# Sparse attention and routed experts on one Trainium2 core: more transposes by DMA, some near rows issued by GpSimd, expert 1's loads released

## The chip, the cores and the metric

The kernel runs on one core of a Trainium2 chip. The core has five engines that run side by side and are tied together by semaphores: TensorE (matmuls and transposes, PE in the profile), VectorE (DVE), ScalarE (ACT), GpSimd (POOL) and SyncE (SP, which here only issues DMAs). Each takes its own instructions in program order. DMAs are issued by an engine and carried out by 16 DMA engines that all queues share. The metric is the device time of one execution in microseconds (us).

## The reference

Two stages. Attention over 4 batches, 8 heads, 768 positions, head dimension 64: every query sees the keys less than 16 positions away, and beside them 24 block summaries (the maximum of the keys and the mean of the values over blocks of 32):

```python
k_sum = k.reshape(B, H, nb, block, D).max(axis=3)
v_sum = v.reshape(B, H, nb, block, D).mean(axis=3)
scores_l = scale * np.matmul(q, k.transpose(0, 1, 3, 2))
mask_l = np.abs(pos[:, None] - pos[None, :]) < window
scores_s = scale * np.einsum('bhsd,bhnd->bhsn', q, k_sum) + np.log(block)
scores_all = np.concatenate([np.where(mask_l, scores_l, -1e9), scores_s], axis=-1)
a = np.exp(scores_all - max); a = a / (sum + 1e-09)
out = np.matmul(a, np.concatenate([v, v_sum], axis=2))
```

Its output is reshaped to x of 3072 tokens by 512. Then eight experts on all tokens, weighted by a table P that is normalised over rows and columns eight times:

```python
P = np.exp(logits - logits.max())            # logits = x @ w_gate
for _ in range(8):
    P /= P.sum(1, keepdims=True) + 1e-09; P /= P.sum(0, keepdims=True) + 1e-09; P *= N / E
for e in range(E):
    out += P[:, e:e + 1] * (np.maximum(x @ w1[e], 0.0) @ w2[e])
```

## The kernel before

*Pairs.* Attention is done for 16 pairs of heads, i = 0 to 15, four to a batch. Pairs 0 to 3 are taken in halves. From pair 4 on, a pair is one unit of work (`pair_start` and `pair_whole`), and these pairs are what the change touches. A pair goes through these steps:

- GpSimd issues the loads of its keys and queries (`load_qk`, tiles kst and qst, two DMAs each) and of its values (`load_v`, tile vx). They cast from float32 to bfloat16.
- Keys and queries are transposed into kT and qT. Up to pair 11 TensorE does it (`tr`, L305, six 128x128 transposes each) and ScalarE or VectorE copies the result out of PSUM. From pair 12 on SyncE issues a DMA transpose from SBUF to SBUF (`tr_dma`, L310).
- `key_max` and `block_sums` make the block summaries; `block_out` writes the summary values into rows 0 to 63 of the tile Ve.
- `near_values` copies, with four small DMAs (L362, L364), the 16 first and last rows of each block of 128 values into rows 64 to 127 of Ve, where they serve as the neighbours across the block's edge. SyncE issues them.
- `scores` (L334, two halves), `score_exp`, `masks`, `edges` and `summary_exp` make the weights; `values` (two halves) makes the weighted sums: six matmuls of a block with its own values (L406, tile vx), then three that add summaries and near rows (L412, tile Ve). `normalize` divides.
- The outputs go into xT, the transposed input of the experts: by TensorE and a copy (`to_xT`, L517, and `x_out`), for pairs 10 to 14 by a DMA transpose of SyncE (`x_dma`, L314).

*Expert 0* starts while attention still runs: `expert0` works on 384 tokens at a time, in eight hidden tiles of four matmuls each (`hidden_mm`, L200) and three projections of eight matmuls (`project_mm`, L210, each issued as two halves). They fill TensorE between the steps of attention.

*The order.* The kernel is scheduled by its own planner, class `Plan`, when the program is built. Every step is a unit with an engine, a cost, what it depends on, a priority and a lag: the time after its end until its result is taken to be there. The planner gives each engine a fixed order of instructions from these numbers; the hardware then runs each engine's order as it stands, and a unit that is early or late in reality doesn't change it. In this order expert 0's tiles stand between units of attention on TensorE.

*GpSimd's loads* form a chain of their own (`load`, with `last[0]`): pair after pair, then expert 1's weights, four pieces of w1 (`load_w1`, L176, two DMAs of 128 KB each) and w2 (`load_w2`, L187, 1 MB). In front of expert 1's stands a hold (L818 to L822): four one-element copies of GpSimd that read qT of pairs 12 to 15, and so wait until the DMA transposes of these pairs have landed. Tile pools set other waits: V_e has two buffers, so near rows of pair i wait for the weighted sums of pair i-2; vx has six, so the values of pair 15 wait for the sums of pair 9.

*After attention* the routing table is normalised beside the rest of expert 0 and the first group of expert 1; then experts 1 to 7 run through a fixed loop up to the end of the kernel. The planner's part ends at about 170 us.

The units that the change re-plans, in the version before:

```python
if i >= 12:
    U["tr", i, z] = U["kT", i, z] = add("SP", 1.25, lambda z=z: tr_dma(i, z), ...)
...
if 10 <= i < 15:
    U["xt", i] = U["x", i] = add("SP", 1.25, lambda: x_dma(i), ...)
```

Of the kernel before, what the change touches and what calls it, by code (L numbers as in the profile page):

```python
# [10 lines left out]
BF16 = mybir.dt.bfloat16  # L11
# [22 lines left out]
class Plan:  # L34
# [12 lines left out]
    def add(self, eng, cost, fn, deps=(), prio=0.0, opens=(), uses=(), lag=0.0):  # L47
        u = Unit(eng, cost, fn, [d for d in deps if d is not None], prio, list(opens), lag)
        for b in list(opens) + list(uses):
            b.users.append(u)  # L50
        if uses and eng != "PE":
            u.prio -= 100.0
        self.waiting.append(u)
        return u
# [62 lines left out]
def kernel(  # L117
# [10 lines left out]
    nc = tc.nc  # L128

    B, H, S, D = q.shape  # L130
    G = S // 128
# [6 lines left out]
    NP = (B * H) // 2  # L138
    PB = H // 2
    SCALE = 1.0 / float(D) ** 0.5  # L140
    W = 16
# [4 lines left out]
    VD = D + 1  # L146
# [68 lines left out]
    NB = PB  # L215
    NE = 2
# [7 lines left out]
    attn = early.enter_context(tc.tile_pool(name="attn", bufs=1))  # L224
    aps = early.enter_context(tc.tile_pool(name="aps", bufs=1, space=PSUM))
    if True:

        ident = attn.tile([128, 128], BF16, name="ident")
        held = attn.tile([1, 1], BF16, name="held")
        band = attn.tile([128, LIVE], BF16, name="band")  # L230
        m_blk = attn.tile([128, G, 64], BF16, name="m_blk")
        qT = [attn.tile([128, W + S + W], BF16, name=f"qT{i}") for i in range(NB)]
        kT = [attn.tile([128, S], BF16, name=f"kT{i}") for i in range(NB)]
# [10 lines left out]
        add = plan.add  # L244
# [51 lines left out]
        def tr(i, z, tag):  # L296
            st = at.pop(("st", i, z))
            t = at["t", i, z] = bank(tag, "tkq", BF16)
            for g in range(G):
                if i < PB:  # L300
                    for j in range(2):
                        nc.tensor.transpose(t[64 * j:64 * j + 64, g * 128:(g + 1) * 128],
                                            st[:, j, g, :], ident)
                else:
                    nc.tensor.transpose(t[:, g * 128:(g + 1) * 128],  # L305
                                        st[:, g, :, :].rearrange("p j d -> p (j d)"), ident)

        def tr_dma(i, z):
            r, st = i % NB, at.pop(("st", i, z))
            nc.sync.dma_start_transpose(out=(kT[r][:], qT[r][:, W:W + S])[z].rearrange("c (g t) -> c g t", g=G),  # L310
                                        in_=st[:].rearrange("p g j d -> p (g j d)"))
# [45 lines left out]
        def near_values(i):  # L357

            sv, ve = v_x[i % NQ], V_e[i % NE]
            for j in range(2):  # L360
                c0, q0 = VD * j, 64 + 32 * j
                nc.sync.dma_start(out=ve[q0 + W:q0 + 2 * W, 1:G, c0:c0 + VD],  # L362
                                  in_=sv[128 - W:128, j, 0:G - 1, :])
                nc.sync.dma_start(out=ve[q0:q0 + W, 0:G - 1, c0:c0 + VD],  # L364
                                  in_=sv[0:W, j, 1:G, :])

        def scores(i, h):
            sg = at["sg", i, h] = banks2("sg")
            for s in range(HG):
                for j in range(2):  # L370
                    score_mm(i, sg[:, j, s * LIVE:(s + 1) * LIVE], j, HG * h + s, 0, LIVE)
# [244 lines left out]
        U = {}  # L616
        last = [None, None]
# [19 lines left out]
        def pair_start(i, prio):  # L637
            o = i - NB
            war_k = [U.get(("S", o, 0)), U.get(("S", o, 1)), U.get(("km", o))]
            war_q = war_k[:2] + [U.get(("ss", o, 0)), U.get(("ss", o, 1))]  # L640
            tag = "m" if i < PB else "a"
            for z in range(2 if i >= PB else 1):
                if i >= 12:
                    U["tr", i, z] = U["kT", i, z] = add("SP", 1.25, lambda z=z: tr_dma(i, z),
                                                        [U["kq"[z], i]] + (war_k, war_q)[z], prio, lag=5.0)
                    continue
                buf = Buffer(tag)
                U["tr", i, z] = add("PE", 0.4, lambda z=z: tr(i, z, tag),
                                    [U["kq"[z], i], U["ident"]] + (war_k, war_q)[z]
                                    + [U["tr", i, 0] if z else U.get(("S", i - 1, 1 if i > PB else 0))],  # L650
                                    prio, opens=[buf])
                U["kT", i, z] = add({"ACT": 0.8} if z == 0 else {"ACT": 0.8, "DVE": 0.95},
                                    0, lambda z=z: tr_out(U["kT", i, z].on, i, z), [U["tr", i, z]], prio,
                                    uses=[buf])
            if i < PB:
                query_half(i, 0, prio)
            U["km", i] = add("DVE", 0.95, lambda: key_max(i), [U["kT", i, 0]] + war_q[2:], prio)
            buf = Buffer("a")
            U["vs", i] = add("PE", 0.4, lambda: block_sums(i),
                             [U["v", i]] + ([U.get(("A", i - NE, 1))] if i >= PB else []), prio + 0.01, opens=[buf])  # L660
            U["Vs", i] = add("DVE", 0.36 if i < PB else 0.84, lambda: block_out(i), [U["vs", i]],
                             prio + 0.01, uses=[buf])
# [37 lines left out]
            return U.get((what, n % PB, n // PB)) if n >= 0 else None  # L700

        def pair_whole(i, prio):
            U["near", i] = add("SP", 2.5, lambda: near_values(i), [U["v", i], U.get(("A", i - NE, 1))], prio,
                               lag=1.9)
            for h in range(2):
                buf = Buffer("s")
                U["S", i, h] = add("PE", 0.28, lambda h=h: scores(i, h),
                                   [U["kT", i, 0], U["kT", i, 1], U.get(("ed", i - 2))], prio, opens=[buf])
                U["X", i, h] = add("ACT", 0.97, lambda h=h: score_exp(i, h), [U["S", i, h]], prio, uses=[buf])
                U["mk", i, h] = add("DVE", 0.56, lambda h=h: masks(i, h),  # L710
                                    [U["X", i, h], U.get(("A", i - 2, 1))], prio)
            U["ed", i] = add("DVE", 0.78, lambda: edges(i),
                             [U["X", i, 0], U["X", i, 1], U["mk", i, 1], U.get(("A", i - NE, 1))], prio)
            bufs = [Buffer("a"), Buffer("a")]
            U["ss", i, 0] = U["ss", i, 1] = add("PE", 0.22, lambda: summaries2(i),
                                                [U["km", i], U["kT", i, 1], U.get(("A", i - NE, 1))], prio,
                                                opens=bufs)
            for h in range(2):
                U["sx", i, h] = add("ACT", 0.46, lambda h=h: summary_exp(i, h), [U["ss", i, h]], prio,
                                    uses=[bufs[h]])  # L720
            for h in range(2):
                buf = Buffer("a")
                U["A", i, h] = add("PE", 0.4, lambda h=h: values(i, h),
                                   [U["mk", i, h], U["ed", i], U["sx", i, h], U["Vs", i], U["near", i]],
                                   prio, opens=[buf])
                U["no", i, h] = add("DVE", 0.68, lambda h=h: normalize(i, h),
                                    [U["A", i, h], U.get(("xt", i - 2))], prio, uses=[buf])
            if 10 <= i < 15:
                U["xt", i] = U["x", i] = add("SP", 1.25, lambda: x_dma(i), [U["no", i, 0], U["no", i, 1]], prio,
                                             lag=4.5)  # L730
            else:
                buf = Buffer("a")
                U["xt", i] = add("PE", 0.35, lambda: to_xT(i), [U["no", i, 0], U["no", i, 1]], prio, opens=[buf])
                U["x", i] = add({"ACT": 0.8, "DVE": 0.9}, 0, lambda: x_out(U["x", i].on, i), [U["xt", i]], prio,
                                uses=[buf])
# [55 lines left out]
        c0 = add("DVE", 3.8, constants, [], -5.0)  # L791
# [11 lines left out]
        for i in range(PB, NP):  # L803
# [3 lines left out]
            if i % PB == PB - 1:  # L807
# [7 lines left out]
                    zero.extend(U["w2d"])  # L815
                expert0(b * S, xs)
                expert0(b * S + HS, xs)
        def hold():  # L818
            for r in range(12 % NB, NB):
                nc.gpsimd.tensor_copy(out=held[0:1, 0:1], in_=qT[r][0:1, W:W + 1])  # L820

        last[0] = add("POOL", 0.3, hold, [last[0]] + [U["kT", i, 1] for i in range(12, NP)])  # L822
        for i in range(4):
            load(("w1n", i), lambda i=i: load_w1(1, i), 0.85, 1.3)
        load("w2n", lambda: load_w2(1), 0.85, 5.0)
# [13 lines left out]
    if True:  # L839
# [351 lines left out]
        for n in range(LAG, len(groups)):  # L1191
            g0, q0 = g, q
            g = group(*groups[n])
            q = pair(*groups[n - LAG])
            e, j, i = groups[n]
# [48 lines left out]
        last = [pair(*groups[len(groups) - LAG + n], spare=bool(n % 2), c1_at=c1s[n], tail=True) for n in range(LAG)]  # L1244
# [6 lines left out]
        A, B, C, D = last  # L1251
# [42 lines left out]
```

## Time and profile before

| | |
|---|---|
| median of 3 runs | 676.4 us (675.85 to 677.23) |
| the profiled execution | 675.13 us, its span 673.4 us |
| granted TensorE clock over the span | 0.999 |
| TensorE busy, 26.5 to 116 us | 89.00 of 89.50 us |
| VectorE / ScalarE busy there | 76.33 / 66.43 us |
| GpSimd DMA issues in attention | 0.75 to 1.05 us each |
| SyncE issue of a near row / of a DMA transpose | 0.59 / 1.21 to 1.95 us |
| landing of kT's, qT's, xT's DMA transposes after issue (median, range) | 5.2 (2.7 to 6.0), 3.6 (2.8 to 4.5), 4.9 (2.8 to 8.4) us |
| landing of Ve's near rows after issue | 5.0 (1.9 to 6.7) us |

How to read the lines in what follows. A group or timeline line starts with its time: in a timeline, the start in us from the span's start, then the length, the engine, the source line, the operation, the tile written <- the tiles read, the number of instructions, and in brackets how long the engine had been idle before it and what ended the wait. A q after an engine's name is its sequencer: an SPq or POOL DMA line is the issue of a DMA, not its transfer. The view of stretches gives for each stretch its length and then busy time and number of instructions of PE, of PE's weight loads, of DVE, ACT and POOL, the granted clock, the DMA engines' share and GB/s. The view of waits gives engine, line, what it waited for, us in total, times, and the longest.

### The profile page before, as it was taken

The page shows a single profiled execution, that of the slowest core. Times are in us where ns is not written, and L with a number is a line of the kernel's source. Part 1 is how long each engine was busy: PE and PEld are TensorE (multiplying, and loading weights), DVE is VectorE, ACT ScalarE, POOL GpSimd, SP SyncE. Part 2 cuts the span into 40 slices and gives each one's busy share as a digit, 9 for nine tenths or more (in the row PEclk, how much of TensorE's full clock was granted, in tenths as well). Part 3 has the DMA queues.
Part 4 walks back from the last instruction along what each step waited for, and adds up shares of the span by engine and source line. Part 5 has one row for each costly group of instructions (what it writes and reads, how often), then busy time and mean ns, then how long its engine had stood idle before and what let it go on. Part 6 is the DMA issues. An engine that isn't in the chain of part 4 may idle for free.

```text
span 673.4 us, 13531 instructions
## 1 busy us (share of the span) xinstructions
PE 663.9 (99%) x5111; PEld 434.8 (65%) x5111; DVE 580.2 (86%) x1433; ACT 402.5 (60%) x783; POOL 131.5 (20%) x177
## 2 busy tenths in 40 slices
PE   8999999999999999999999999999999999999996
PEld 4666655555666666666666666666666666666665
DVE  6878889777799988998899988998899889998885
ACT  4777776565777765555655565555555555556552
POOL 8599622122101010201010010101020101100001
PEclk9999999999999999999999999999999999999999
DMA  9999959000513060311422050405031141201224
GB/s 115 190 147 145 151 85 172 2 1 1 79 11 37 1 79 1 36 14 21 59 22 28 1 78 9 40 1 79 1 33 17 20 60 20 30 0 48 82 91 158
DMA packets 124018, 36.46 MB, mean 54 GB/s; under 512 B 110384, under 2 KB 121136, under 8 KB 123952
## 3 DMA queue, kind: packets, MB, share of 16 engines
q0 software_dynamic: 104672, 26.22, 41.8%
q1 hardware_dynamic: 18464, 8.83, 5.6%
q8 instruction: 40, 0.66, 0.4%
q10 hardware_dynamic: 816, 0.54, 0.2%
q14 instruction: 26, 0.21, 0.1%
HBM read 52.45 MB, written 6.29 MB: 87 GB/s over the span
## 4 chain that ended last, share of the span: by engine, by line
PE 93%; DVE 4%; DMA 1%; POOL 1%; issue 1%; ACT 0%; DVEq 0%; ACTq 0%
PE xy L913 36%; PE pg L907 16%; PE pa L907 11%; PE pb L907 11%; PE hps L200 6%; PE yps L210 6%; PE sg L334 1%; DMA kst<-in_k_dram 1%; DVE hf L857 1%; PE tkq L305 1%; PE vs L342 1%; PE av L406 1%; PE av L412 1%; PE ss L430 1%; PE tx L517 0%
## 5 line engine op out<-in xcount | busy, mean ns | idle before, releaser
L913 PEld LDWEIGHTS <-hf 128*128 128x128 f16 x2352 | 230.1, 98 | 95.6 <-issue 0.5
L913 PE MATMUL xy<-w,hf 128*128 128x256 f16 x1312 | 183.4, 273 | 0.0
L913 PE MATMUL xy<-ws,hf 128*128 128x256 f16 x984 | 147.6, 273 | 0.1
L191 ACT ACTIVATE hf<-pg 128x512 f16<-128x512 f32 x84 | 50.2, 597 | 150.8 <-PE pg L907 150.8
L1049 DVE SCALAR_TENSOR_TENSOR out_acc<-xy,P_sb,out_acc 128x512 f32<-128x512 f32 x164 | 115.1, 744 | 2.1 <-PE xy L913 2.1
L854 DVE TENSOR_TENSOR hf<-hf 128x512 f16<-128x512 f16 x252 | 100.3, 424 | 8.8
L907 PE MATMUL pa<-xT,w 128*128 128x512 f16 x336 | 99.9, 379 | 0.0
L907 PEld LDWEIGHTS <-w 128*128 128x128 f16 x672 | 65.8, 98 | 44.4 <-issue 1.1
L857 DVE TENSOR_TENSOR hf<-pb,c 128x512 f16<-128x512 f32 x84 | 58.1, 692 | 38.5 <-PE pb L907 32.4
L176 POOL DMA_DIRECT2D w<-in_moe_w_dram x56 | 41.7, 754 | 220.6 <-PE pg L907 192.0
L907 PEld LDWEIGHTS <-ws 128*128 128x128 f16 x504 | 49.3, 98 | 25.3
L941 ACT COPY c<-pg 128x512 f32<-128x512 f32 x84 | 49.2, 586 | 22.4 <-PE pg L907 22.4
L857 DVE TENSOR_TENSOR hf<-pg,c 128x512 f16<-128x512 f32 x84 | 57.2, 681 | 0.8 <-PE pg L907 0.8
L926 ACT COPY pg<-pa 128x512 f32<-128x512 f32 x84 | 47.9, 570 | 4.8
L191 ACT ACTIVATE hf<-pa 128x512 f16<-128x512 f32 x84 | 50.6, 602 | 0.0
L907 PE MATMUL pg<-xTs,w 128*128 128x512 f16 x168 | 50.0, 379 | 0.2
L907 PE MATMUL pg<-xT,w 128*128 128x512 f16 x168 | 50.0, 379 | 0.1
L907 PE MATMUL pb<-xT,ws 128*128 128x512 f16 x168 | 50.0, 379 | 0.0
L907 PE MATMUL pb<-xTs,ws 128*128 128x512 f16 x168 | 50.0, 379 | 0.0
L907 PE MATMUL pg<-xTs,ws 128*128 128x512 f16 x168 | 50.0, 379 | 0.0
L934 ACT COPY c<-pb 128x512 f32<-128x512 f32 x84 | 49.8, 592 | 0.0
L200 PE MATMUL hps<-xT,w 128*128 128x384 f16 x256 | 48.6, 326 | 0.0
(141 smaller groups left out, 820.1 us busy)
## 6 DMA issues: line engine op xcount, KB each, us to landing
w<-in_moe_w_dram POOLq DMA_DIRECT2D x8, 1024.0 KB, 8.9
w<-in_moe_w_dram POOLq DMA_DIRECT2D x56, 128.0 KB, 3.5
out_dram<-out_acc SPq DMA_DIRECT2D x20, 256.0 KB, 2.0
qst<-in_q_dram POOLq DMA_DIRECT2D x32, 96.0 KB, 5.7
vx<-in_v_dram POOLq DMA_DIRECT2D x16, 192.0 KB, 6.5
kst<-in_k_dram POOLq DMA_DIRECT2D x24, 96.0 KB, 5.9
w<-in_moe_w_dram POOLq DMA_DIRECT2D x2, 512.0 KB, 8.6
kst<-in_k_dram POOLq DMA_DIRECT2D x4, 192.0 KB, 5.1
```

Source lines behind the costliest of these rows:

```text
L176: nc.gpsimd.dma_start(out=t[:, :, h, :], in_=moe_w1[e].rearrange("(dk p) f -> p dk f", p=128)[:, :, f:f + 128])
L191: nc.scalar.activation(out=out, in_=in_, func=AF.Relu, bias=0.0, scale=1.0)
L200: nc.tensor.matmul(hp[:, 0:n], lhsT=w1s[e][:, dk, 128 * f:128 * (f + 1)], rhs=xT[:, dk, t0:t0 + n], start=(dk == 0), stop=(dk == KD - 1))
L210: nc.tensor.matmul(yp[:], lhsT=h[:, f, c * 128:(c + 1) * 128], rhs=w2s[e][:, f, :], start=(f == 0), stop=(f == KF - 1))
L854: nc.vector.tensor_tensor(out=out, in0=in0, in1=in1, op=ALU.subtract)
L857: nc.vector.tensor_tensor(out=out, in0=in0, in1=in1, op=ALU.add)
L907: nc.tensor.matmul(bank[:], lhsT=w[:, dk, :], rhs=x[:, dk, :], start=start and dk == 0, stop=dk == KH - 1, skip_group_check=True)
L913: nc.tensor.matmul(bank, lhsT=a(f)[:, 128 * c:128 * (c + 1)], rhs=w[:, f, :], start=start and f == 0, stop=f == FH - 1, skip_group_check=True)
L926: nc.scalar.copy(out=B["g"][:], in_=B["a"][:])
L934: nc.scalar.copy(out=B["c5"][:], in_=B["b"][:])
L941: nc.scalar.copy(out=B["c2"][:], in_=B["g"][:])
L1049: nc.vector.scalar_tensor_tensor(out=acc, in0=src, scalar=P_sb[:, t, e:e + 1], in1=acc, op0=ALU.mult, op1=ALU.add)
```

## The change

Five edits, all in what the planner is given, and one removed step:

- Keys and queries of pairs 10 and 11 are transposed by DMA as well (before: from pair 12 on); the lag in the plan is 6 (5.0).
- Outputs of pairs 8 and 9 go by DMA transpose as well (before: 10 to 14); lag 5 (4.5).
- Near rows of pairs 12 to 15 are issued by GpSimd instead of SyncE, with a plan cost of 3.6 for the four; the lag of all near rows is 2.2 (1.9).
- The hold in front of expert 1's loads is gone, with its tile.

```diff
-                nc.sync.dma_start(out=ve[q0 + W:q0 + 2 * W, 1:G, c0:c0 + VD],
+                eng = nc.gpsimd if i >= 12 else nc.sync
+                eng.dma_start(out=ve[q0 + W:q0 + 2 * W, 1:G, c0:c0 + VD],
                                   in_=sv[128 - W:128, j, 0:G - 1, :])
-                nc.sync.dma_start(out=ve[q0:q0 + W, 0:G - 1, c0:c0 + VD],
+                eng.dma_start(out=ve[q0:q0 + W, 0:G - 1, c0:c0 + VD],
                                   in_=sv[0:W, j, 1:G, :])
...
-                if i >= 12:
+                if i >= 10:
                     U["tr", i, z] = U["kT", i, z] = add("SP", 1.25, lambda z=z: tr_dma(i, z),
-                                                        [U["kq"[z], i]] + (war_k, war_q)[z], prio, lag=5.0)
+                                                        [U["kq"[z], i]] + (war_k, war_q)[z], prio, lag=6)
...
-            U["near", i] = add("SP", 2.5, lambda: near_values(i), [U["v", i], U.get(("A", i - NE, 1))], prio,
-                               lag=1.9)
+            U["near", i] = add(*(("POOL", 3.6) if i >= 12 else ("SP", 2.5)), lambda: near_values(i),
+                               [U["v", i], U.get(("A", i - NE, 1))], prio, lag=2.2)
...
-            if 10 <= i < 15:
+            if 8 <= i < 15:
                 U["xt", i] = U["x", i] = add("SP", 1.25, lambda: x_dma(i), [U["no", i, 0], U["no", i, 1]], prio,
-                                             lag=4.5)
+                                             lag=5)
...
-        def hold():
-            for r in range(12 % NB, NB):
-                nc.gpsimd.tensor_copy(out=held[0:1, 0:1], in_=qT[r][0:1, W:W + 1])
-
-        last[0] = add("POOL", 0.3, hold, [last[0]] + [U["kT", i, 1] for i in range(12, NP)])
         for i in range(4):
             load(("w1n", i), lambda i=i: load_w1(1, i), 0.85, 1.3)
         load("w2n", lambda: load_w2(1), 0.85, 5.0)
```

With the new numbers the planner also orders the engines anew. On SyncE, from the near rows of pair 8 on, the changed program has: transposes of pair 10, near rows of 9, transposes of 11, near rows of 10, output of 8, transposes of 12 and 13, near rows of 11, output of 9, transposes of 14, output of 10, transposes of 15, outputs of 11 to 14. On GpSimd, after the values of pair 15: the eight w1 loads and the w2 load of expert 1, then the near rows of pairs 12, 13, 14 and 15, then the routing table's steps. On TensorE 36 transposes are gone, and the tiles of expert 0 stand at other places between the units of attention.

More of the change, by code (lines that the diff above doesn't have):

```diff
@@ L228 @@
         ident = attn.tile([128, 128], BF16, name="ident")
-        held = attn.tile([1, 1], BF16, name="held")
         band = attn.tile([128, LIVE], BF16, name="band")
```

## The prediction, made before the changed kernel was run

> **What bounds the kernel now.** I read the busy table first, then the stretch the change touches cut out of the trace, then the waits of TensorE and of GpSimd, then the order of time on the three queues concerned. In the page and in the cut:
>
> ```profile
> PE 663.9 (99%) x5111; PEld 434.8 (65%) x5111; DVE 580.2 (86%) x1433; ACT 402.5 (60%) x783; POOL 131.5 (20%) x177
> ...
> 74.00:116.00 42.00, 42.00 (x443) 24.65 (x440) 37.41 (x102) 30.20 (x51) 12.70 (x19) 1.00 1.19 136
> ```
>
> TensorE is busy in all 42.00 us from 74 to 116 us, where everything that the change touches happens, and at full clock (1.00). It takes its instructions in order and has no gap to give. So work taken from TensorE there shortens the kernel by its own length, and a wait put in front of one of its instructions lengthens it by the whole wait. In the view of who waited for whom, no line of TensorE in this stretch waits for a DMA. GpSimd does:
>
> ```profile
> POOL held L820 <- DMA qT<-qst: 16.1, 4, 7.2
> ```
>
> These 16.1 us are the hold that is taken out. In order of time GpSimd shows its last load of attention, the four copies that hold, and expert 1's loads:
>
> ```profile
> 79.98 1.02 POOL L274 DMA_DIRECT2D vx<-in_v_dram  x1 [2.23 <-PE av L412]
> ...
> 98.00 0.18 POOL L820 COPY held<-qT 1x1 bf16<-1x1 bf16 x1 [7.21 <-DMA qT<-qst]
> 98.46 5.95 POOL L176 DMA_DIRECT2D w<-in_moe_w_dram  x8 [0.28 <-issue]
> 104.34 0.95 POOL L187 DMA_DIRECT2D w<-in_moe_w_dram  x1
> ```
>
> The view of the tile w, cut to these loads, has their way from issue to landing. The longest belongs to the load of w2 (cut to 104.0 to 105.5 us, the last small load shows 5.3 and w2 12.3), so w2 landed at 104.3 + 12.3 = 116.6 us; cut to its own issue, the first one landed in 3.7 us, at 102.1 us:
>
> ```profile
> DMA to landing us min/median/max: 3.7/5.0/12.3
> ```
>
> And TensorE, at the place that matters below, pair 12's weighted sums (the L412 matmuls read Ve, which the near rows fill):
>
> ```profile
> 100.54 0.35 PE L406 MATMUL av<-vx,em 128*128 128x65 bf16 x6
> 100.73 0.34 PE L412 MATMUL av<-Ve,Ee 128*128 128x130 bf16 x3
> ```
>
> There they followed the tile before without a wait: pair 12's near rows were issued by SyncE from 88.64 to 91.15 us, and the tile view of Ve for that window gives 1.9 us to landing.
>
> **What the Trainium skill says.** (1) "DMA: Bandwidth & Descriptors", section on SWDGE, HWDGE and iDMA: GpSimd's descriptors go to a ring of which one context is allocated, while SyncE's go to another queue of the same 16 engines, served in turn. The trace agrees: all GpSimd DMAs stand under one queue, q0, SyncE's under q1. (2) Same page, section "Two DMAs through the same engine are not ordered": within one queue of an engine descriptors start in order. The trace fits: w2, last of nine, took 12.3 us where the first took 3.7. (3) Same page, "Queues, rings and completion order": a completion write lands after every earlier write of its engine, across queues. The trace fits: near rows of SyncE landed in 1.9 us when GpSimd loaded nothing (88 to 92 us) and in 4.4 to 6.1 us beside expert 1's loads (101 to 110 us). (4) "TensorE: Matmul & The Clock Gate", Part 1: after an idle window of about 3.4 us the clock is halved until a busy one has passed. Here TensorE's last matmul starts at 667.91 and ends by 668.5 us; the clock record falls to 0.50 at 672.6 us, 4.1 us later.
>
> **What is taken from TensorE.** By the order of time, from the start of one unit to the next: queries' and keys' transposes of pair 10 took 76.44 to 77.20, 0.76 us; pair 11's 81.97 to 82.65, 0.68 us; the output transposes of pair 8 took 74.81 to 75.14, 0.33 us; pair 9's 81.22 to 81.65, 0.43 us. Sum 2.20 us. The evacuations that go with them (six 128x768 copies on ScalarE and VectorE, 0.56 to 0.80 us each) stood beside a full TensorE, as did the hold's copies, and are worth nothing. If nothing else were late, the gain would be 2.2 us.
>
> **What is put on SyncE.** Six DMA transposes of 1.2 to 1.5 us of issue each, minus the near rows of four pairs (16 issues of 0.6 us). Pair 10's transposes can go at 61.7 us, when near rows of pair 8 are out (61.02 + 0.62) and the loads have landed; with the 4.5 to 5.7 us that pair 12's took, they are there by 70 us and the scores of pair 10 start at about 75.9. Pair 11's go behind near rows of pair 9 (66.2 to 68.7), are there by 77, and are read at about 81. Both hidden. Then near rows of pair 10 (to 76.5), the output of pair 8 (1.3), four transposes of pairs 12 and 13, to about 83.9, and only then near rows of pair 11, against 81.16 in the profile: the last is issued at about 85.8 and, with 4.4 to 6.1 us, lands between 90.2 and 91.9. The sums of pair 11 come, without a wait, at 93.28 - 2.20 - 0.65 (one hidden tile now placed after them) = 90.4. So 0 to 1.5 us may be lost there; I take 0.5.
>
> **What moves on GpSimd.** In the changed program the nine loads of expert 1 stand directly behind the values of pair 15, and the near rows of pairs 12 to 15 stand behind the loads, also on GpSimd. The values of pair 15 wait for the sums of pair 9. On TensorE these now have before them 2.42 us more (a hidden tile 0.65, half a projection 0.86, two score units 0.63, the summaries 0.28) and 1.09 less (transposes of pair 10, outputs of pair 8), so the load goes at 79.98 + 1.33 = 81.3 instead of 79.98; it took 6.5 us to land, so 87.8. The loads are issued from 82.3, their data is queued behind it. In the profile the nine landings ran from 102.1 to 116.6, 14.5 us; with the first one 1 us after the values (the eight small loads landed 1 us apart: 98.46 + 3.7 to 103.6 + 5.3), w2 lands at 88.8 + 14.5 = 103.3. Two bounds: if the values don't hold them up, 18.1 us after the first issue as in the profile (116.6 - 98.46), 100.4; if the seven transposes that SyncE now sends in this time (pair 9's output to pair 11's) rather than three cost their whole size, 4 x 0.197 MB at the 174 GB/s that the cut from 108 to 117 us shows, 4.5 us, 107.8. In the profile both kinds of traffic together moved more than loads alone (211 GB/s from 82 to 84 us against 144 from 58 to 82), so a part of this; I take 105.
>
> Near rows of pair 12 are issued once GpSimd is past the loads, and in the program every GpSimd DMA also waits for the landing of the eighth before it: about 89.5 to 93. Their descriptors then stand in q0 behind w2's, on the same engines. They land with w2, at 105.
>
> Sums of pair 12: in the changed order TensorE has before them 2.20 less and also lacks the last hidden tile (98.17 to 98.82, 0.65 us) and a projection (98.82 to 100.54, 1.72), which come after: it is there at 100.54 - 2.20 - 2.37 = 96.0, or 96.5 with pair 11's half microsecond, and passes L406 at once. L412 waits from 96.2 to 105.1, 8.9 us. Behind it in TensorE's queue stands everything else: scores of pair 14, hidden tiles and projections of expert 0; none can pass, so all 8.9 us are lost. (The 0.5 of pair 11 falls into this wait: the landing does not move with it.) Against the profile: 105.1 - 100.73 = 4.4 late, plus the 2.37 that are still owed, **6.7 us late**. Nothing further adds: the last near row of pair 13 may be issued only when w2 has landed, 105.7, landing at 108, but its sums come 6 us after those of pair 12, at 111; pairs 14 and 15 are issued after the sums of 12 and 13 into an empty ring. Earlier landing of expert 1's weights buys nothing: in the profile no TensorE or VectorE wait names their DMA.
>
> **The clock.** 8.9 us of idle are more than the 4.1 after which the record falls. At the start of the profile the clock was half until 7.03 us, TensorE having begun at 1.05. Half speed for 3.4 (the skill's window) to 6 us after the wait costs half of that, 1.7 to 3.0 us; bound below 0 if the record should not fall. I take 2.0. Sum: 8.7 us. The profiled execution took 675.1 us (span 673.4 and 1.7 around it), so 683.8; the median of the runs is 1.3 higher, 676.4, so **685.1**, and I say 685.
>
> **Rivals.**
> - *Near rows pass the weights* (another ring, or small DMAs interleaved): issued by 93.3, landing in 1.9 to 6.1 us, 95.2 to 99.4, against 96.2. TensorE waits 0 to 3.2 us: -2.2 to +1.0, 674.2 to 677.4, most likely 674.5. This is the faster side; it decides if near rows land by about 98.4. For it: only 10 KB each, and the change's own due time for them is 2.2 us. Against: nine loads in the profile landed strictly one behind the other.
> - *A short wait*: the weights land at the lower bound, 100.4, and the clock falls late or not at all: 100.5 - 100.73 + 2.37 = +2.1, and up to 2 of clock: 678.5 to 680.5. For it: the profile's own 18.1 us. Against: the values of pair 15 ahead, and more transposes beside.
> - *SyncE is what is late*: near rows of pair 12 arrive in time, but those of pair 11, behind four transposes, hold its sums by 1.5: -2.2 + 1.5 = -0.7, 675.7. For it: 4.4 to 6.1 us to landing under load. Against: only true if the first rival is.
>
> **How the numbers follow.** Near rows behind the weights, long wait: 0.75, 680.5 to 690 (680.5 without any clock cost and w2 at 102.8; 107.8 with 3.0 of clock gives +12.5, 688.9). Short wait: 0.08. Near rows pass: 0.12 (0.09 faster, 0.01 the same, 0.02 slower). SyncE late: 0.05 (0.03 faster, 0.02 the same). A measurement of this kernel tells about 0.2%, 1.4 us, from no change. Faster 0.12, same 0.03, slower 0.85. The range 677.5 to 690 leaves out the faster cases (0.17 at most) and the upper tail.
>
> **What would show it.** In the profile of the changed kernel: the near rows of pair 12 issued by GpSimd at 89 to 93 us with 10 us or more to landing; a wait of TensorE at L412 for the DMA Ve<-vx of 5 to 10 us around 96 us; a clock record of 0.50 within it or behind it; SyncE's transposes of pairs 10 and 11 with no TensorE wait behind them; 36 fewer transposes on TensorE. It is wrong if the near rows land within 6 us, or if TensorE has no wait above 2 us between 85 and 110 us.

## The result and the profile after

| | before | after |
|---|---|---|
| median | 676.82 us (675.85 to 679.24, 4 runs) | 696.73 us (696.42 to 698.21, 4 runs) |
| ratio | | 1.0293, 95% interval 1.0262 to 1.0324 |
| the profiled execution: span | 673.4 us | 694.6 us |
| granted TensorE clock over the span | 0.999 | 0.982 |

The changed kernel is slower by 19.9 us. The prediction said slower, at the right place, but by 8.7 us, less than half of it. The busy times of the page and the cut of the stretch from 74 to 116 us, the two views that the prediction began with, now of the changed kernel:

```profile
PE 666.7 (96%) x5075; PEld 434.4 (63%) x5075; DVE 581.1 (84%) x1434; ACT 398.8 (57%) x776; POOL 138.5 (20%) x189
```

```profile
74.00:116.00 42.00, 24.90 (x218) 12.62 (x217) 20.58 (x57) 16.76 (x27) 16.04 (x23) 0.80 1.63 153
```

36 transposes are gone from TensorE (5111 instructions before, 5075 now). But where it was busy in all 42.00 us it now works 24.90, at a mean clock of 0.80, and the DMA engines carry 153 GB/s instead of 136. The view of who waited for whom, TensorE alone, 60 to 140 us:

```profile
PE av L412 <- DMA Ve<-vx: 15.3, 1, 15.3
PE sg L333 <- DMA qT<-qst: 3.6, 1, 3.6
```

And the order of time at those places:

```profile
89.82 0.58 PE L333 MATMUL sg<-qT,kT 64*128 64x160 bf16 x6 [3.60 <-DMA qT<-qst]
...
98.44 0.88 POOL L187 DMA_DIRECT2D w<-in_moe_w_dram  x1 [0.59 <-DMA w<-in_moe_w_dram]
100.11 0.56 POOL L362 DMA_DIRECT2D Ve<-vx  x1 [0.79 <-PE ss L430]
...
102.15 0.35 PE L406 MATMUL av<-vx,em 128*128 128x65 bf16 x6
...
117.83 0.50 PE L412 MATMUL av<-Ve,Ee 128*128 128x130 bf16 x3 [15.33 <-DMA Ve<-vx]
```

The long wait is the one that the prediction described: pair 12's sums, L412, for near rows that GpSimd issued behind expert 1's weights. It lasts 15.3 us instead of 8.9, and it ends at 117.83 us, not at 105.1. The second wait, 3.6 us for the queries of pair 12, was not foreseen at all. The tile views give the ways to landing. First w2 alone, second the four near rows of pair 12, third the values of pair 15 (6.5 us before):

```profile
L187 POOL DMA_DIRECT2D w<-in_moe_w_dram x1: 883/883/883, 98.4 to 98.4; - x1
...
DMA to landing us min/median/max: 18.5/18.5/18.5
```

```profile
DMA to landing us min/median/max: 13.5/15.4/17.0
```

```profile
DMA to landing us min/median/max: 14.3/14.3/14.3
```

So w2, issued at 98.44, landed at 116.9, and the near rows between 117.2 (100.11 + 17.0) and 117.7 (104.18 + 13.5), directly behind it. What made all of it late stands in the chain of work that ended last, cut to this stretch (start, length, what):

```profile
78.30 13.51 DMA kst<-in_k_dram
...
92.10 11.80 DMA w<-in_moe_w_dram
...
104.18 13.51 DMA Ve<-vx
...
117.83 0.50 PE av L412 x3
```

From 78 us on the chain holds nothing but DMAs of GpSimd's queue, three in a row of 11.8 to 13.5 us each. (Each GpSimd DMA waits for the landing of the eighth before it: w2 was issued at 98.44, just after the first of the eight w1 loads had landed at 98.14. So late landings also stretch the issue of the rest: expert 1's nine loads were issued in 6.8 us before, and took from 83.2 to 99.3 us now.) The reason for the slow landings is in the DMA view of 61 to 86 us, from the first added transpose to the time at which pair 15's values landed before. Per queue it gives packets, MB, and the packets' times added up as a share (over 100% where they overlap). First before, then after:

```profile
DMA packets 25697, 3.58 MB, mean 143 GB/s; under 512 B 25693, under 2 KB 25693, under 8 KB 25693
...
q0 software_dynamic: 21496, 2.71, 186.3%
q1 hardware_dynamic: 4197, 0.81, 23.6%
```

```profile
DMA packets 23399, 3.60 MB, mean 144 GB/s; under 512 B 23396, under 2 KB 23396, under 8 KB 23396
...
q0 software_dynamic: 16989, 2.14, 154.3%
q1 hardware_dynamic: 6407, 1.41, 53.7%
```

The DMA engines move as much as before, 144 GB/s against 143, but SyncE's queue q1 has 0.60 MB more of it and GpSimd's queue q0 0.57 MB less. What the transposes took, the loads lost. That is what was missed. (The packet times that the page gives for the whole span are no price: SyncE's queue goes from 5.6% of 673.4 us to 7.5% of 694.6, but with the hold alone taken out it goes to 6.2% of 677.8 with the same 8.83 MB as before, so they also grow with what runs beside.)

**The account.** TensorE ran pair 12's L412 at 117.83 instead of 100.73: 17.1 us late. From there to the end it took 694.6 - 117.83 = 576.8 us instead of 673.4 - 100.73 = 572.7: 4.1 more, made of tiles of expert 0 that had been put behind this point (2.37 in the prediction) and of half clock up to 122.9 us (2.5), less 0.8 whose source is open. 17.1 + 4.1 = 21.2, the difference of the spans.

### The profile page after: what moved, and what is told of

It is laid out like the page before. It is cut to its first block, busy times and chain, and to the rows that moved or that the text cites. A ratio compares the mean times of both kernels' runs of the same rounds, so it can differ in the third digit from the quotient of the medians.

```text
span 694.6 us, 13463 instructions
## 1 busy us (share of the span) xinstructions
PE 666.7 (96%) x5075; PEld 434.4 (63%) x5075; DVE 581.1 (84%) x1434; ACT 398.8 (57%) x776; POOL 138.5 (20%) x189
## 4 chain that ended last, share of the span: by engine, by line
PE 87%; DMA 8%; DVE 2%; POOL 1%; issue 1%; ACT 0%; DVEq 0%; SPq 0%; POOLq 0%; ACTq 0%
PE xy L908 36%; PE pg L902 15%; PE pb L902 10%; PE pa L902 10%; PE yps L210 5%; PE hps L200 4%; DMA kst<-in_k_dram 4%; DMA Ve<-vx 3%; DMA w<-in_moe_w_dram 2%; PE sg L333 1%; PE av L479 1%; PE vs L341 1%; PE tkq L304 0%; POOL vx L273 0%; PE av L412 0%
## 5 line engine op out<-in xcount | busy, mean ns | idle before, releaser
L908 PEld LDWEIGHTS <-hf 128*128 128x128 f16 x2352 | 230.1, 98 | 95.6 <-issue 0.5
```

Source lines behind the costliest of these rows:

```text
L908: nc.tensor.matmul(bank, lhsT=a(f)[:, 128 * c:128 * (c + 1)], rhs=w[:, f, :], start=start and f == 0, stop=f == FH - 1, skip_group_check=True)
```

## The experiments

Two questions: is the lateness of the near rows the queue behind w2, and what moved w2 from the predicted 103 to 105 us to 117? The theory is that both kinds of added transposes take the DMA engines from GpSimd's loads, byte for byte or worse, from 61 us on. The rivals differ from run to run. Ratios and losses are against runs of before on the same chip (medians 674.86, 675.72 or 676.94 us). With every edit the planner also orders the engines anew, so no run changes one thing alone; what the order itself costs was not tested. Line numbers shift from kernel to kernel (L411 to L415 are all the sums' last three matmuls, L412 of before). In the waits sg are scores, av sums, ss the summaries, xs the outputs before their transpose, lp the routing logits.

### The parts put together and taken out

**Near rows back on SyncE** (the changed kernel otherwise):

```diff
-                eng = nc.gpsimd if i >= 12 else nc.sync
+                eng = nc.sync
...
-            U["near", i] = add(*(("POOL", 3.6) if i >= 12 else ("SP", 2.5)), lambda: near_values(i),
-                               [U["v", i], U.get(("A", i - NE, 1))], prio, lag=2.2)
+            U["near", i] = add("SP", 2.5, lambda: near_values(i), [U["v", i], U.get(("A", i - NE, 1))], prio,
+                               lag=2.2)
```

> The changed kernel with the near rows of pairs 12 to 15 issued by SyncE again; transposes, outputs and the missing hold stay. Queue theory (near rows wait in GpSimd's queue behind w2, and that queue is late because the added DMA transposes share the DMA engines with the loads): TensorE's 15.3 us wait at L412 of pair 12 goes, with the second fall of the clock; the values of pair 15 still land near 96 us and the 3.6 us wait of pair 12's scores stays, so 679 to 685 us. Rival (SyncE is the late queue: near rows behind its transposes): the wait at L412 stays, only with SyncE as issuer, above 690 us.

688.5 us, ratio 1.0209 (1.0170 to 1.0247), above what was expected. The wait at the sums fell to 0.3 us; another came:

```profile
PE sg L333 <- DMA qT<-qst: 10.1, 2, 6.7
...
PE av L411 <- DMA Ve<-vx: 0.3, 1, 0.3
```

The 6.7 us are the scores of pair 14, whose queries were issued at 99.2 us by SyncE and took 13.5 us to land, 112.7, beside w2 (landed 115.7). So near rows on GpSimd make the one wait, but a free w2 delays SyncE's transposes as well. Here even near rows of SyncE landed with w2: those of pair 13, issued from 102.1 us on behind these transposes, landed 12.6 to 13.6 us later, from 115.7 to 116.6.

**The hold put back** (near rows on GpSimd, added transposes):

```diff
+        def hold():
+            for r in range(12 % NB, NB):
+                nc.gpsimd.tensor_copy(out=held[0:1, 0:1], in_=qT[r][0:1, W:W + 1])
+
+        last[0] = add("POOL", 0.3, hold, [last[0]] + [U["kT", i, 1] for i in range(12, NP)])
```

> The changed kernel with the hold in front of expert 1's loads put back. The planner now puts the near rows of pairs 12 to 14 ahead of the loads and those of pair 15 behind them. Queue theory: the long wait moves from pair 12 to pair 15 (its near rows land with w2, some 15 us after the hold ends), pair 12's wait at L412 is under 3 us; 685 to 695 us. Rival (no queue effect, the missing hold let loads collide with the transposes): with the hold all long waits go, 675 to 680 us.

687.53 us, ratio 1.0187 (1.0167 to 1.0206). The wait moved to pair 15, whose near rows now stand behind w2 (landed 126.3; they 126.5 to 127.2), 5.7 us of the 7.8:

```profile
PE av L413 <- DMA Ve<-vx: 7.8, 2, 5.7
PE sg L334 <- DMA qT<-qst: 3.5, 1, 3.5
```

**The transposes alone** (the kernel before with `i >= 10`, lag 6, and `8 <= i < 15`, lag 5):

> The kernel before with only the two transpose edits (queries and keys from pair 10, outputs from pair 8); near rows by SyncE and the hold as before. If the added DMA transposes share the engines byte by byte with GpSimd's loads (six times 0.197 MB at about 140 KB per us, 8.4 us), the values of pair 15 land at 94 to 97 us instead of 86.5, and TensorE waits 3 to 4 us for pair 12's queries; with the clock 678 to 683 us. If instead expert 1's loads, let go early, made the transposes late, there is no such wait here and the gain of 2.2 us shows: 674 to 675 us.

680.03 us, ratio 1.0078 (1.0063 to 1.0093). The wait for the queries of pair 12 stays as it was in the changed kernel, though near rows and hold are those of before; the values of pair 15 needed 14.4 us to land, against 6.5:

```profile
PE sg L334 <- DMA qT<-qst: 3.5, 1, 3.5
```

The DMA view of 61 to 86 us is that of the changed kernel too: 143 GB/s in all, 2.10 MB by q0, 1.42 MB by q1. So the added transposes alone turn an expected saving of 2.2 us into a loss of 5.2 (680.03 - 674.86, the median of before on that chip), and delay the loads.

**Expert 1's loads planned last** (the changed kernel, the loads behind the near rows of pair 15):

```diff
+        last[0] = add("POOL", 0.0, None, [last[0], U["near", NP - 1]])
         for i in range(4):
             load(("w1n", i), lambda i=i: load_w1(1, i), 0.85, 1.3)
```

> The changed kernel, but with expert 1's loads put behind the near rows of pair 15 in GpSimd's order (no hold; the near rows stay with GpSimd). Queue theory: the near rows of pair 12 are no longer behind w2 but behind the values of pair 15, landing at 97 to 100 us; the wait at L412 is under 4 us, the wait of pair 12's scores (3.6 us) stays: 678 to 684 us. Rival (GpSimd's issue of near rows is slow by itself, one in eight DMAs in flight): the near rows still land 10 us or more after issue and the wait stays above 8 us, 688 us or more.

679.1 us, ratio 1.0062 (1.0045 to 1.0079). GpSimd still issues the near rows; with no weights in front of them those of pair 12 landed by 99.1 us, and no line of L412 is left among the waits:

```profile
PE sg L333 <- DMA qT<-qst: 3.2, 1, 3.2
```

So with the weights behind the near rows the loss is 4.2 us (679.1 - 674.86) instead of 19.9: most of it hangs on the weights standing in front. This run takes away both things that they do there, near rows behind them and SyncE's transposes beside them; the near rows back on SyncE, which takes away only the first, still lose 13.6 us (688.5 - 674.86).

Its trace also has two near rows of 10 KB that were issued at the same time, 85.8 us, by GpSimd (pair 12) and by SyncE (pair 11):

```profile
L362 POOL DMA_DIRECT2D Ve<-vx x1: 564/564/564, 85.8 to 85.8; - x1
...
DMA to landing us min/median/max: 12.5/12.5/12.5
```

```profile
L362 SPq DMA_DIRECT2D Ve<-vx x1: 1337/1337/1337, 85.8 to 85.8; - x1
...
DMA to landing us min/median/max: 7.3/7.3/7.3
```

GpSimd's landed at 98.3, directly behind the values of pair 15 (97.9), which stood in front of it in the same queue. So 5.2 us go with the queue. SyncE's own took 7.3 us, behind transposes in its queue and beside the loads; in the kernel before, 1.9 us were enough while GpSimd loaded nothing.

### One part of the change at a time

**Near rows on GpSimd alone** (before, with the near rows of the change):

> The kernel before with one part of the change: near rows of pairs 12 to 15 issued by GpSimd; transposes and hold as before. In the new order near rows of pairs 12 and 13 stand in front of the hold, those of 14 and 15 behind expert 1's w2. Theory (near rows land when the weights in front of them in the same queue have landed): near rows of pairs 12 and 13 land in time; those of pair 14 land with w2, near 117 us, and TensorE waits at L413 for pair 14 about 4 us, with 1.5 to 3 us of half clock behind it: 679 to 682. Rival (near rows are late because of the added transposes, not because of the weights): no such wait, 675 to 676.

680.38 us, ratio 1.0071 (1.0054 to 1.0088), as the theory had it. Near rows of pairs 12 and 13, in front of the hold, landed 1.9 to 2.9 us after their issue. Those of pair 14 were issued behind w2:

```profile
L363 POOL DMA_DIRECT2D Ve<-vx x2: 612/624/637, 104.1 to 105.2; - x2
...
DMA to landing us min/median/max: 11.0/11.5/12.1
```

They landed from 116.19 us on, w2 at 115.93, and TensorE waited 3.7 us. The same 10 KB, issued by the same engine, take 2 us or 12. The first also had less beside them on the DMA engines, so this run alone doesn't tell the queue from the engines that all share.

**No hold alone** (before without the hold):

> The kernel before with one part of the change: the hold in front of expert 1's loads is taken out; transposes and near rows as before. Theory: the loads then run from about 81 to 98 us beside the transposes of pairs 13 to 15 and SyncE's near rows of pairs 11 to 13, each of which comes some 4 us later; there was 5 us or more of slack, so no wait of TensorE above 1 us: 674 to 676. Rival (the hold alone protects the transposes, as the 6.7 us wait for pair 14's queries with the near rows back on SyncE suggests): a wait of TensorE for qT of pair 13 or 14 of 3 us or more, 678 to 682.

680.09 us, ratio 1.0069 (1.0054 to 1.0084): the theory of slack was wrong. No line of TensorE waits for queries, so the rival's wait isn't there either; it is the outputs:

```profile
DVE xs L509 <- DMA xT<-xs: 2.9, 1, 2.9
...
PE ss L429 <- DVE xs L509: 2.0, 2, 1.6
```

The output transpose of pair 10, issued by SyncE at 93.6 us, took 11.1 us and landed at 104.7, with w2 (104.5). VectorE waits for it before it may write the next output into the tile, its later work waits behind, and TensorE waits for VectorE. The run shows two more things. The hold is worth 4.4 us (680.09 - 675.72, the median of before on that chip). And without added transposes w2 landed at 104.5 us.

**Keys and queries alone** (before with `i >= 10` and lag 6):

> The kernel before with one part of the change: keys and queries of pairs 10 and 11 by DMA transpose; outputs, near rows and hold as before. Theory (the added transposes share the 16 DMA engines with GpSimd's loads and so delay them and the transposes behind them): four transposes of 0.197 MB between 61 and 75 us add about 4.5 us to the loads behind them, so the values of pair 15 land near 92 us (86.5 in before, 96.4 with both kinds of transposes) and the queries of pair 12 near 87; TensorE's wait for them is under 2 us or none; 674 to 677 us. Rival (it is the number of transposes in SyncE's own queue, with the outputs, that makes pair 12 late, and the loads have no part in it): values of pair 15 still land near 87 us, and the gain of 1.44 us of TensorE is kept whole, 673.4.

683.15 us, ratio 1.0114 (1.0095 to 1.0133), outside both. The values of pair 15 took 10.7 us to land, between before (6.5) and both kinds of transposes (14.4). No wait for queries; instead near rows and VectorE were late:

```profile
PE lp L531 <- DVE xs L510: 2.3, 1, 2.3
PE av L412 <- DMA Ve<-vx: 1.4, 1, 1.4
```

The profiled execution, the slowest of the four (684.67), also lost some 4 us in its first 25 us, where the edit changes nothing, so times on its axis are not set against those of before; why this part alone costs more than both kinds together was not settled.

**Outputs alone** (before with `8 <= i < 15` and lag 5):

> The kernel before with one part of the change: outputs of pairs 8 and 9 by DMA transpose; all else as before. Theory: two transposes of 0.197 MB around 78 us, when most of GpSimd's loads of attention are through, cost the loads 2 us at most; no wait of TensorE; the 0.76 us of transposes saved on TensorE come through: 674.0 to 674.8, 0.4 to 0.8 less than before. Rival (the outputs alone, sent in front of the transposes of pairs 12 and 13 on SyncE, make pair 12 late): a TensorE wait for the queries of pair 12 of 2 us or more, 677 or more.

681.63 us, ratio 1.0091 (1.0077 to 1.0105), a miss as well (the profiled execution, 683.68, is the slowest of the five). The loads were not delayed (values of pair 15 landed in 6.3 us), and no queries were late. Here SyncE came to the last transposes later, the hold let the weights go at 105.6 instead of 98.5 us, and the output of pair 14, issued at 113.6, landed with w2, 12.7 us later, at 126.3:

```profile
PE lp L531 <- DMA xT<-xs: 3.9, 2, 3.3
PE tx L517 <- DVE xs L510: 1.3, 2, 0.9
```

**The same with w2 held** until the output of pair 14 has landed:

```diff
+        def hold2():
+            nc.gpsimd.tensor_copy(out=held[0:1, 0:1], in_=xT[0:1, 14 % PB, 14 // PB * S:14 // PB * S + 1])
+
+        last[0] = add("POOL", 0.1, hold2, [last[0], U["x", 14]])
         load("w2n", lambda: load_w2(1), 0.85, 5.0)
```

> The run with outputs alone by DMA from pair 8 on, which took 681.63, with w2 held until the output transpose of pair 14 has landed. Theory (that transpose came 12.7 us after its issue because it stood beside w2, and its wait and the half clock behind it are the whole loss): it lands within 6 us, no wait of the routing logits above 1 us, 674 to 676. Rival (the loss there comes from VectorE, whose sums wait for the outputs of pairs 12 and 13 beside w1): waits of TensorE for VectorE's xs of 2 us or more stay, 678 or more.

677.53 us, ratio 0.9988 (0.9968 to 1.0008). That output landed in 4.3 us, the wait is 0.4, and the loss of 0.9% is gone. A wait of 2.3 us for VectorE's xs is left, as the rival had it, so both had a part; the hoped-for gain can't be told from nothing.

### The size, and the clock

**The changed kernel without its added transposes** (`i >= 12`, `10 <= i < 15`, lags 5.0 and 4.5):

> The changed kernel without its added transposes: keys and queries by DMA from pair 12, outputs from pair 10, as before; near rows of pairs 12 to 15 by GpSimd and no hold, as changed. This is the case that the prediction's sum really describes. Theory (the added transposes are what put the landing of w2 and the near rows from 105 to 117 us): w2 lands near 104.5, as it did with the hold alone taken out (104.47), the near rows of pair 12 directly behind it; the wait at pair 12's sums is 6 to 8 us and the kernel takes 8 to 11 us more than before: 683 to 687. Rival (the weights and near rows are late by GpSimd's own queue, with transposes having no part): landing near 115 us or later, a wait of 14 us or more, 693 to 697.

682.78 us, ratio 1.0076 (1.0055 to 1.0097), against 676.94 for before, whose runs scattered more on this chip (674.41 to 684.09 in 60). The order of time at the sums of pair 12, and the landing of their near rows:

```profile
99.30 0.35 PE L406 MATMUL av<-vx,em 128*128 128x65 bf16 x6
105.38 0.50 PE L412 MATMUL av<-Ve,Ee 128*128 128x130 bf16 x3 [5.73 <-DMA Ve<-vx]
```

```profile
DMA to landing us min/median/max: 13.6/14.9/15.4
```

w2 landed at 104.3, the near rows at 104.5 to 105.3, and the wait ends at 105.38 where the prediction had 105.1. The wait is slightly under the expected 6 to 8 us because TensorE came later (99.3, not 96.2), and the loss is 5.8 us, not 8 to 11. This is the answer to the second question: with the transposes of before, w2 and the near rows are there at 105; the six added ones put them at 117.

**TensorE kept busy in front of pair 12's scores** (both kinds of transposes in before, with 15 matmuls of zeros):

```diff
+            for _ in range(15 if (i, h) == (12, 0) else 0):
+                nc.tensor.matmul(sg[:, 0, :], lhsT=zeros[:], rhs=zeros[:, None, :].to_broadcast([128, 4, 128]),
+                                 start=True, stop=True)
```

> The kernel before with all added transposes (as in the run with the transposes alone), and 15 matmuls of 128x512 put in front of the scores of pair 12, whose results are overwritten: TensorE is then busy in the 3.5 us in which it otherwise waits for the queries of pair 12. They do no work for the output. Theory (the 6.8 us at half clock behind that wait come from the idle time and cost 3.4 us, as much as the wait): the clock record stays at 1.0 there, and the time is 1.5 to 3.5 us less than the 680.03 with the transposes alone: 676.5 to 678.5. Rival (the clock record says little of the work's speed, or the clock falls for another reason): no gain or a loss, 680 to 682.

681.7 us, ratio 1.0066 (1.0046 to 1.0085), against 1.0078 (1.0063 to 1.0093) without them, on another chip: no gain that can be told, and the intervals don't exclude one of about 2 us. The clock stayed up, as the stretches of both show, first with the transposes alone, then with the matmuls:

```profile
86.00:90.00 4.00, 0.51 (x8) 0.29 (x6) 3.81 (x12) 0.00 (x0) 0.18 (x1) 0.89 1.92 117
90.00:97.00 7.00, 7.00 (x41) 2.63 (x38) 0.27 (x2) 3.92 (x6) 0.18 (x1) 0.58 1.63 142
```

```profile
86.00:90.00 4.00, 4.00 (x27) 1.84 (x26) 3.78 (x13) 0.11 (x1) 0.00 (x0) 1.00 1.87 119
90.00:97.00 7.00, 4.43 (x39) 2.13 (x39) 1.65 (x3) 3.79 (x6) 0.36 (x2) 1.00 1.56 139
```

But TensorE used it only to arrive sooner at the next thing that wasn't there, the near rows of pair 11, which SyncE's queue landed at 97.1. In its waits a second one stands, at the routing logits (L534), for an output transpose that landed with w2 (131.2 and 131.5 us):

```profile
97.14 0.38 PE L415 MATMUL av<-Ve,Ee 128*128 128x130 bf16 x3 [2.70 <-DMA Ve<-vx]
```

```profile
PE av L415 <- DMA Ve<-vx: 2.7, 1, 2.7
PE lp L534 <- DMA xT<-xs: 2.5, 1, 2.5
```

With the half clock those sums ran at 96.77 without a wait. Behind the new wait the clock fell all the same, from 98.2 to 101.6 us, and pair 12's sums came at 104.28, later than the 102.31 with the transposes alone. So neither theory's reason holds: the clock does follow the idle time, but here keeping it up in front of a DMA that ended last moved the wait and the half clock on. The second wait blurs the result, and the profiled execution (685.08) is one of the slowest of the 20.

**A version meant to beat before**: keys and queries from pair 11 (`i >= 11`, lag 6), outputs from pair 8, w2 held as above.

> A version meant to beat the kernel before: keys and queries by DMA from pair 11 on (not 10), outputs from pair 8 on, near rows and hold as before, and a second hold in front of w2 alone, until the output transpose of pair 14 has landed (so that no output transpose stands beside the 1 MB of w2). Theory: two transposes less in front of the loads than in the changed kernel, so the queries of pair 12 land near 87 us with a wait of at most 1 us; 1.4 us of TensorE's transposes are saved: 673.5 to 675.5. Rival (one more pair is already too much, since the loads of the next pairs are delayed byte for byte): a wait of 1.5 us or more for the queries of pair 11 or 12, half clock behind it, 677 to 681.

679.3 us, ratio 1.0029 (1.0012 to 1.0046). The queries of pair 12 landed at 87.0, as expected, and no wait for queries is left, so the rival's wait isn't there; yet 1.4 us less of transposes brought no gain. Between 30 and 130 us its profile has 1.4 us of TensorE waits in all; before 30 us, where the edit changes nothing, it has 4.7 us, against 2.4 in before. So where the other runs lose their small rest is not settled. No version beat the kernel before.

## Why the prediction was wrong

- **The sign, the place and the mechanism** held. The rival that near rows pass the weights fell: in four kernels (changed, hold put back, near rows alone, no added transposes) they landed with it, the first 0.2 to 0.3 us and the last of the pair 0.7 to 0.9 us behind w2.
- **The step that failed** is the landing of the near rows, "I take 105", in its bounds too (100.4 to 107.8): it was 117.2 to 117.7. It failed in its first input, the values of pair 15: "it took 6.5 us to land, so 87.8". They were issued at 82.2, against a predicted 81.3, but took 14.3 us and landed at 96.4, 8.6 us late. From there w2 took another 20.5 us, to 116.9, where the prediction had 17.2: 3.3 us more (without the added transposes 17.5, from 86.8 to 104.3). The prediction had counted the added transposes only from there on, as "4 x 0.197 MB at the 174 GB/s" = 4.5 us beside the weights, and then taken a part of that, because both kinds of traffic had moved "211 GB/s" in a cut of 2 us; over the 25 us from 61 to 86 the total did not rise at all (143 and 144 GB/s). The transposes of pairs 10 and 11, which run from 61 us on, were asked only whether they themselves come in time ("Both hidden"), never what they do to the queue beside them. The run without added transposes gives 105.38 for the end of the wait, so this term was right for a kernel without them, and 12.4 us short with them. That it agrees to 0.3 us there has luck in it: 1.7 us of the 105 were meant for transposes that this run doesn't have. No other term of the sum is needed: with 117.8 in place of 105.1 it gives 117.8 - 100.73 + 2.37 + 2.0 = 21.4 us, against 21.2 between the spans.
- **The Trainium skill** had the warning on the page that was cited: "DMA: Bandwidth & Descriptors", section "Issuing engines are not separate DMA queues", says that DMAs of all engines run on the same 16 DMA engines and interleave. The trace agrees, and gives the price: from 61 to 86 us SyncE's queue gained 0.60 MB and GpSimd's lost 0.57 at the same total. The prediction used this for near rows and four transposes of SyncE beside the weights and forgot it for transposes beside the loads of attention.
- **"Both hidden"** held for pairs 10 and 11 themselves (no TensorE wait for their keys or queries) and failed one pair on: queries of pair 12 were issued at 79.75 and took 9.9 us (4.5 before), and TensorE waited 3.6. In the changed kernel this wait lies inside the longer one, as TensorE only arrived later at L412 (102.15, predicted 96.0); with the long wait gone it is what remains.
- **The near rows of pair 11**, put at 90.2 to 91.9 and 0.5 us, landed at 94.3 to 95.9 and were covered by the same 3.6 us.
- **The 2.2 us**: the 36 transposes are gone, and the sums of pair 10 came at 85.07 instead of 87.09. But they came at 85.85 without the added transposes too, so a part of this is the new order; how much of the 2.2 us was saved is not shown. Whatever was saved was lost in the first wait behind.
- **The clock**, put at 2.0 us behind the wait: 5.0 us of half speed after 117.83 (to 122.87), so 2.5. A second drop, from 88.7 to 95.6 us, was in front of the long wait and cost nothing there.
- **The hold**: "Earlier landing of expert 1's weights buys nothing" held (no run gained from it), but its removal has a price of its own, which the prediction gave as nothing: 4.4 us (680.09 - 675.72) for the hold alone; the waits in its trace start at an output transpose that landed with w2.
- **Two smaller slips.** That w2, last of nine, took 12.3 us and the first load 3.7 says little of their order, as w2 has eight times the bytes (1024 KB, 128 KB). And w2 at 102.8 without clock cost gives 102.9 - 100.73 + 2.37 = 4.5 us by the prediction's own sum, so 680.9, not 680.5.

## What to carry to other kernels

A DMA that is taken off a busy engine's hands is paid for by every transfer that shares the DMA engines, so price it by what is queued behind and beside it from its issue on, not only by whether it arrives in time itself. Before small transfers with a due time are put on a queue, look what stands in front of them there; a large load that nobody needs soon belongs behind them, and a wait that keeps it back can be worth more than it seems. When a path of several DMAs decides, shortening one wait in front of the last one can gain nothing (nor did keeping the clock up there show a gain here); look for the transfer that ends last.

## What was not expected of the hardware

- Output transposes of SyncE landed together with a 1 MB load of GpSimd that had been issued before them, though the queues differ: at 104.7 against w2's 104.5 (no hold alone), and 126.3 against 126.6 (outputs alone). With w2 held back the second took 4.3 us instead of 12.7. Near rows of SyncE that were issued while w2 was under way came before it in two kernels (landed 112.1 to 114.0 against w2's 116.6 in before, 99.8 to 101.2 against 104.5 with no hold alone) and with it in one (near rows back on SyncE). What decides was not settled.
- Five of the six added transposes had landed when pair 15's values did; the sixth, issued at 89.8 us, was under way. The five have 0.98 MB, by estimate 6.8 us at the 144 GB/s of 61 to 86 us, but the values landed 9.9 us later (86.5 to 96.4); 2.2 us of this are their later issue. Outputs alone did not delay them (6.3 us to landing); keys and queries alone did (10.7 us).
- The clock fell after shorter idle times than the 4.1 us that the prediction measured and the 3.4 it quoted: behind waits of 2.7 us (TensorE kept busy) and 2.3 us (outputs with w2 held), to 0.50 for about 3.4 us. With no hold alone it fell from 106.6 to 110.0 us, behind waits of 1.6 and 0.4 us. With w2 held, the stretch behind the wait:

```profile
114.50:117.80 3.30, 3.30 (x13) 1.54 (x12) 2.83 (x7) 0.98 (x2) 0.00 (x0) 0.50 1.60 150
```
